# Sketched attention with a squared-ReLU feed-forward: four dummy matmuls ahead of the k features, w_o in rows of four, all casts of w_in on GpSimd

## The chip, the cores and the metric

The kernel runs on one core of a Trainium2 chip. The metric is device time in microseconds (us); of the kernel before there are three runs. A core has five engines that work side by side, each through its own queue in program order: TensorE (PE, with the weight loads shown as PEld), VectorE (DVE), ScalarE (ACT), GpSimd (POOL) and SyncE (SP, which here issues nearly all DMAs). They wait for each other by semaphores. SBUF is the core's working memory with 128 partitions, PSUM holds what PE writes.

## The reference

Attention with a degree-two sketch, then a feed-forward layer with a squared ReLU:

```python
# q, k, v: (4, 4, 1088, 32); S1, S2: (8, 32); w_in: (128, 2048); w_out: (2048, 128)
def phi(x):                       # 64 features of each row
    a = einsum('rd,bhsd->bhsr', S1, x)
    b = einsum('rd,bhsd->bhsr', S2, x)
    return einsum('bhsi,bhsj->bhsij', a, b).reshape(..., 64)
kv  = einsum('bhsf,bhsd->bhfd', phi(k), v)
z   = sum(phi(k), axis=2)
num = einsum('bhsf,bhfd->bhsd', phi(q), kv)
den = einsum('bhsf,bhf->bhs', phi(q), z)[..., None] + 1e-06
x   = (num / den).transpose(0, 2, 1, 3).reshape(4352, 128)
h   = maximum(x @ w_in, 0)
out = h * h @ w_out
```

The sum over the 2048 columns of h may be taken in any order, as long as column f of w_in meets row f of w_out.

## The kernel before

The feed-forward part is most of the work. The 4352 rows of x stand as columns of a tile xT (128 partitions are the model dimension). They are cut into ten chunks of 256 to 512 columns (FC). For each chunk and each of 16 blocks of 128 hidden features (d0 to d15) there is a first matmul pg (`ffn1`, L583: weights are a block of w_in, data are xT), a relu on ACT (L592, into gt), a square on ACT (L600) or DVE (L602, into g), and a second matmul that accumulates in PSUM (`ffn2`, L621, tile po; for the last chunk L616), whose weights are a block of w_o. Blocks are taken in units of one or more; the first chunk has the units u0 and u1 with one block each, then units of two blocks. po is transposed (L625) and stored by SP (L635).

The weights of both matmuls are loaded in four chunks of 512 columns: w_in arrives as float32 in w_in32 (`load_wi`, L204), and a cast (`cast_wi`, L665) writes it as the type that the matmul reads into w_in; w_o is loaded straight (`load_wo`, L209). Chunk c holds blocks 4c to 4c + 3. In w_o, block d of chunk c holds rows 128 (4c + d) to 128 (4c + d) + 127 of w_out, one row per partition, so each partition of a chunk's transfer takes four pieces of 128 floats (512 bytes). Casts 0, 1 and 3 stand ahead of the copies of the kv sums, cast 2 behind them; 0, 1 and 2 are on ACT, 3 is on POOL.

The attention part makes xT piece by piece. Batch 0 is written out by hand and comes first, in three pieces of q (256, 384 and 448 rows); the rest is placed by a planner (`_Order`) which fixes each engine's order when the kernel is built, from costs given for each step. The hand-written start goes like this:

- SP issues the loads of S1, S2, k, the first q, eight of v (L195), then w_in 0, w_o 0, the second q, and w_in and w_o 1 to 3 in turn, the third q, and batch 1's loads.
- PE does five dummy matmuls on constants (`keep_warm`, L672, W0 = 5), the sketch's selection (L683, tile sp), W1 = 2 more dummies, and then the k features kf (`a_kf`, L308), whose data come from DVE's transposes of k (L283). ACT copies half of each (L314), DVE multiplies them to kp (L324).
- PE makes the q features x (`q0`, L732) and sums kp and v into kvp (`a_kv0`, L384). DVE makes block-diagonal forms bd and zm from kvp (L764, L774), and PE the denominators den (L757, L787), and the numerators num (L787). From these DVE makes the first 256 columns of xT (L806 to L811).
- ACT copies kvp to kvt (L782), and a small product to sw (L798); PE replicates kvt (`a_rep`, L427), and ACT copies the result to kv (`a_rep_kv`, L433). After one more dummy (W3 = 1) PE starts on pg.

The second piece of q then goes through the planner's steps: qT (DVE, L289), qc (PE, L296), qt (DVE, L469), pd, dn and rc (DVE, L475, L485, L489), sixteen small copies rd (POOL, L497), shuffles qa and qb (DVE, L506), products qp (DVE, L521), nd (PE, L536), bc (DVE, L546) and xT (DVE, L553). Its 384 columns are the second chunk of the feed-forward part. kT (L277) and kc (L338) are the first steps of batch 1.

Of the kernel before, what the change touches and what calls it, by code (L numbers as in the profile page):

```python
# [14 lines left out]
def _ap(t: bass.AP, p0: int, np_: int, off: int, free):  # L15
    p = list(t.ap)[0]
    return bass.AP(
        t.tensor, t.offset + p0 * p[0] + off, [[p[0], np_]] + [list(d) for d in free]
    )
# [85 lines left out]
def kernel(  # L105
# [11 lines left out]
    nc = tc.nc  # L117
# [6 lines left out]
    NB = 16  # L124
    GT, G2, LA = 4, 6, 3.5
    LU = 4
    W0, W1, W3 = 5, 2, 1
    ND, QT, WI, KL, QL = 2, 3.0, (1.0, 1.9), (30.0, 12.0), 4.0


# [25 lines left out]
    def sb(name, cols, dt=F32, rows=128):  # L156
        return cpool.tile([rows, cols], dt, tag=name, name=name)
# [9 lines left out]
    w_in32, w_o, w_in = sb("w_in32", 2048), sb("w_o", 2048), sb("w_in", 2048, F32R)  # L167
# [39 lines left out]

    def load_wo(eng, c):
        eng.dma_start(  # L209
            _ap(w_o, 0, 128, 512 * c, [[128, 4], [1, 128]]),  # L210
            bass.AP(
                moe_w_out.tensor, moe_w_out.offset + c * 512 * 128,
                [[128, 128], [128 * 128, 4], [1, 128]],
            ),
        )

# [214 lines left out]
    def a_rep_kv(t_, col):  # L431
        kv = st[0, "kv"] = bpool.tile([128, 64 * H], F32, tag="kv", name="kv")
        nc.scalar.copy(  # L433
            _ap(kv, 0, 128, 0, [[32, 4], [128, 2], [1, 32]]),
            _ap(t_, 0, 128, col, [[512, 4], [64, 2], [1, 32]]),
        )
# [225 lines left out]
        store(1)  # L662

    def cast_wi(c):
        (nc.scalar.copy if c < 3 else nc.gpsimd.tensor_copy)(  # L665
            w_in[:, 512 * c : 512 * c + 512], w_in32[:, 512 * c : 512 * c + 512]
        )

    def keep_warm(n, cols=512):
# [16 lines left out]
    nc.scalar.copy(ss[:, :], sp[:, 0:80])  # L686
    load_wi(nc.sync, 0)
    load_wo(nc.sync, 0)
    load_q(nc.sync, 0, 256, 640)
    for c in range(1, 4):  # L690
        load_wi(nc.sync, c)
        load_wo(nc.sync, c)
# [75 lines left out]
            op=mult,  # L768
        )

    for c in (0, 1, 3):
        cast_wi(c)
    a_bd(1)
    nc.vector.tensor_tensor(  # L774
# [24 lines left out]
    nd0(num0, 0)  # L799
    a_rep(x0, 256)  # L800
    a_rep_kv(x0, 256)
    cast_wi(2)
    st["warm"] = psf.tile([128, 512], F32, tag="po", name="warm")
    keep_warm(W3)
    dT0 = wpool.tile([128, 256], F32, tag="dT0", bufs=1, name="dT0")
# [276 lines left out]
```

## Time and profile before

| what | value |
| --- | --- |
| median of 3 runs | 187.65 us (187.32 to 188.25) |
| the profiled execution, its own time | 188.6 us |
| its span | 186.8 us |
| DMA packets, bytes | 24673, 11.25 MB |
| of these under 512 B, under 2 KB | 18000, 23120 |
| cast of w_in, 128x512, on ACT | 0.62 us, three times |
| cast of w_in, 128x512, on POOL | 0.61 us, once |
| w_in transfers, issue to landing | 4.5 to 5.8 us, median 5.2 |
| w_o transfers, issue to landing | 4.7 to 6.2 us, median 5.3 |

A line of the timeline has its start and its length in us, the engine, the line of the kernel, the operation, the tile written and those read, the shape, and how many such operations are merged in it. What stands in brackets is the time for which the engine idled before, and what ended the wait. In the chain that ended last, each step is what released the next one. A record of PE's start-up shows two entries for each float32 matmul.

### The profile page before, as it was taken

To read this page: it belongs to the slowest core of one execution; us is meant where nothing else is said; L and a number is where in the kernel's file an instruction comes from. 1 tells how busy PE (TensorE), PEld (TensorE's weight loads), DVE (VectorE), ACT (ScalarE), POOL (GpSimd) and SP (SyncE) were. 2 spreads that over 40 slices of the span, in tenths; PEclk is the share of its full clock that TensorE was granted. 3 is DMA by queue.
4 is the path that set the end of the run, shared out by engine and by line. 5 is a ranking of instruction groups with operands and counts; after the bars stand their busy time and mean duration, and the time that the engine had idled before them with its cause. 6 is when DMAs were issued, how large, how long until landed. Compare 5 with 4: busy or idle time off the path is not lost.

```text
span 186.8 us, 3886 instructions
## 1 busy us (share of the span) xinstructions
PE 180.5 (97%) x1476; PEld 104.8 (56%) x1476; DVE 119.9 (64%) x254; ACT 136.5 (73%) x265; POOL 33.5 (18%) x154
## 2 busy tenths in 40 slices
PE   7987999999999999999999999999999999999992
PEld 1755866665656556554554555554555555555792
DVE  4856969996995679599626992999334235322420
ACT  3228977967986979499577875796778887877760
POOL 4401602608600000681000002830000000000000
PEclk9999999999999999999999999999999999999999
DMA  5879910110018810000492200002103000300111
GB/s 163 192 224 315 234 51 4 17 14 4 0 21 207 209 15 0 4 0 0 65 279 83 42 0 5 0 0 33 28 0 56 0 0 4 56 0 0 28 28 28
DMA packets 24673, 11.25 MB, mean 60 GB/s; under 512 B 18000, under 2 KB 23120, under 8 KB 24656
## 3 DMA queue, kind: packets, MB, share of 16 engines
q1 hardware_dynamic: 24448, 10.95, 25.0%
q8 instruction: 11, 0.18, 0.5%
q10 hardware_dynamic: 208, 0.07, 0.2%
q14 instruction: 6, 0.05, 0.1%
HBM read 8.78 MB, written 2.23 MB: 59 GB/s over the span
## 4 chain that ended last, share of the span: by engine, by line
PE 90%; SPq 3%; DMA 3%; ACT 1%; issue 1%; DVE 0%; ACTq 0%
PE po L621 60%; PE pg L583 18%; PE nd L536 3%; DMA w_in<-in_moe_w_in_dram 3%; PE kvp L402 2%; PE pol L616 2%; PE po L616 2%; SPq L195 2%; PE qc L296 1%; PE kc L338 1%; SPq L183 0%; SPq L177 0%; PE x L427 0%; ACT gt L592 0%; ACT w_in L665 0%
## 5 line engine op out<-in xcount | busy, mean ns | idle before, releaser
L621 PE MATMUL po<-g,w_o 128*128 128x512 f32 (+3 forms) x288 | 123.8, 548 | 0.0
L592 ACT ACTIVATE gt<-pg 128x512 f32<-128x512 f32 (+3 forms) x145 | 75.3, 569 | 33.1 <-PE pg L583 32.7
L621 PEld LDWEIGHTS po<-g,w_o 128*128 128x128 f32 x288 | 53.0, 189 | 32.4 <-issue 23.9
L583 PE MATMUL pg<-xT,w_in 128*128 128x512 f32 (+3 forms) x160 | 69.4, 517 | 0.5 <-ACT gt L592 0.5
L600 ACT ACTIVATE g<-gt 128x512 f32<-128x512 f32 (+2 forms) x105 | 60.0, 602 | 1.4
L602 DVE TENSOR_TENSOR g<-gt 128x512 f32<-128x512 f32 (+3 forms) x40 | 26.6, 667 | 41.9 <-ACT gt L592 41.3
L583 PEld LDWEIGHTS pg<-xT,w_in 128*128 128x128 f32 x160 | 29.0, 190 | 29.5 <-ACT gt L592 12.5
L443 POOL COPY kv<-kvt 32x64 f32<-32x64 f32 x48 | 12.1, 252 | 64.4 <-DVE kvt L420 62.3
L497 POOL COPY rd<-rc 32x9 f32<-32x9 f32 (+2 forms) x80 | 16.3, 203 | 12.5 <-DVE rc L489 9.1
L506 DVE STREAM_SHUFFLE qa<-qc 128x576 f32<-128x576 f32 (+2 forms) x20 | 11.6, 652 | 0.0
L521 DVE TENSOR_TENSOR qp<-qa,qb 128x576 f32<-128x576 f32 (+2 forms) x20 | 10.8, 605 | 0.0
L355 DVE TENSOR_TENSOR kp<-fs 128x576 f32<-128x576 f32 x12 | 8.4, 752 | 0.1
L469 DVE STREAM_TRANSPOSE qt<-qc 128x576 f32<-128x576 f32 (+2 forms) x10 | 5.8, 614 | 3.9 <-PE qc L296 3.9
L625 DVE STREAM_TRANSPOSE oT<-po 128x512 f32<-128x512 f32 (+3 forms) x9 | 5.9, 652 | 2.4 <-PE po L621 2.4
L536 PE MATMUL nd<-qp,kv 32*32 32x288 f32 (+2 forms) x320 | 6.8, 353 | 0.0
L553 DVE TENSOR_TENSOR xT<-nd,bc 128x576 fp32r<-128x576 f32 (+2 forms) x10 | 5.6, 601 | 1.0 <-PE nd L536 1.0
L546 DVE STREAM_TRANSPOSE bc<-rd 128x576 f32<-128x576 f32 (+2 forms) x10 | 5.8, 605 | 0.4 <-POOL rd L497 0.3
L506 DVE STREAM_SHUFFLE qb<-qc 128x576 f32<-128x576 f32 (+2 forms) x10 | 6.0, 650 | 0.0
L289 DVE STREAM_TRANSPOSE qT<-qn 128x192 f32<-128x192 f32 (+3 forms) x11 | 5.9, 563 | 0.0
L536 PEld LDWEIGHTS nd<-qp,kv 32*32 32x32 f32 x320 | 3.8, 103 | 3.7 <-issue 2.2
L616 PE MATMUL pol<-w_o,g 128*128 128x128 f32 x32 | 5.7, 275 | 0.0
L616 PE MATMUL po<-w_o,g 128*128 128x128 f32 x32 | 5.7, 275 | 0.0
(93 smaller groups left out, 90.7 us busy)
## 6 DMA issues: line engine op xcount, KB each, us to landing
kn<-in_k_dram SPq DMA_DIRECT2D x3, 544.0 KB, 5.5
qn<-in_q_dram SPq DMA_DIRECT2D x3, 544.0 KB, 7.9
vn<-in_v_dram SPq DMA_DIRECT2D x9, 144.0 KB, 4.8
w_in<-in_moe_w_in_dram SPq DMA_DIRECT2D x4, 256.0 KB, 5.2
w_o<-in_moe_w_out_dram SPq DMA_DIRECT2D x4, 256.0 KB, 5.3
out_dram<-oT SPq DMA_DIRECT2D x12, 64.0 KB, 2.0
out_dram<-oT SPq DMA_DIRECT2D x8, 56.0 KB, 2.8
out_dram<-oT SPq DMA_DIRECT2D x8, 48.0 KB, 1.8
```

The source lines that it names most:

```text
L355: nc.vector.tensor_tensor(out=_ap(st[b, "kp"], 0, 128, 64 * NT * h, [[64, NT], [8, 8], [1, 8]]), in0=_ap(fs, 0, 128, o, [[32, NT], [1, 8], ...
L443: nc.gpsimd.tensor_copy(_ap(st[b, "kv"], 32 * c, 32, 64 * h, [[32, E], [1, 32]]), _ap(st["kvt"], 32 * h, 32, 0, [[64, E], [1, 32]]),)
L497: nc.gpsimd.tensor_copy(st[b, "rd", i0][32 * h : 32 * h + 32, n * c : n * c + n], st["rc"][32 * c : 32 * c + 32, n * h : n * h + n],)
L506: nc.vector.stream_shuffle(in_=banks(st[b, "qc", i0], 2 * x, 0, m), out=_ap(st[b, which, i0], 0, 128, 2 * m * x, [[m, 2], [1, m]]), mask=m ...
L521: nc.vector.tensor_tensor(out=st[b, "qp", i0, e][:, r], in0=st[b, f"qa{e}", i0][:, r], in1=st[b, "qb", i0][:, r], op=mult,)
L536: nc.tensor.matmul(nd[32 * h : 32 * h + 32, 512 * c : 512 * c + m], kv[r, o : o + 32], qp[r, m * h : m * h + m], start=(e == 0), stop=(e = ...
L583: nc.tensor.matmul(st["pg", u][:, n * i : n * i + n], w_in[:, 128 * (d0 + i) : 128 * (d0 + i) + 128], xT[:, c0 : c0 + n],)
L592: nc.scalar.activation(gt[:, 0:w], st["pg", u][:, 0:w], Relu)
L600: nc.scalar.activation(g2[:, 0:w], gt[:, 0:w], Square)
L602: nc.vector.tensor_tensor(out=g2[:, 0:w], in0=gt[:, 0:w], in1=gt[:, 0:w], op=mult)
L616: nc.tensor.matmul(po[x // 128][:, 0:128], g[:, x : x + 128], w, start=(d == 0), stop=(d == NB - 1),)
L621: nc.tensor.matmul(po[0][:, 0:n], w, g, start=(d == 0), stop=(d == NB - 1))
```

## The change

Four dummy matmuls instead of two ahead of the k features. The load of w_o takes, in each chunk, four consecutive rows of w_out into each partition (2048 bytes in one piece), so that block j of chunk c holds the rows 512 c + 4 p + j on partition p. To match, the cast of w_in picks the columns 4 p + j of its chunk for block j: its source is read in steps of four floats, its target is written contiguously. All four casts are on GpSimd, in order, ahead of the copies of the kv sums. The order of the other instructions is the same on every engine.

```diff
-    W0, W1, W3 = 5, 2, 1
+    W0, W1, W3 = 5, 4, 1
...
     def load_wo(eng, c):
         eng.dma_start(
-            _ap(w_o, 0, 128, 512 * c, [[128, 4], [1, 128]]),
+            w_o[:, 512 * c : 512 * c + 512],
             bass.AP(
-                moe_w_out.tensor, moe_w_out.offset + c * 512 * 128,
-                [[128, 128], [128 * 128, 4], [1, 128]],
+                moe_w_out.tensor, moe_w_out.offset + c * 512 * 128, [[512, 128], [1, 512]]
             ),
         )
...
     def cast_wi(c):
-        (nc.scalar.copy if c < 3 else nc.gpsimd.tensor_copy)(
-            w_in[:, 512 * c : 512 * c + 512], w_in32[:, 512 * c : 512 * c + 512]
+        nc.gpsimd.tensor_copy(
+            _ap(w_in, 0, 128, 512 * c, [[128, 4], [1, 128]]),
+            _ap(w_in32, 0, 128, 512 * c, [[1, 4], [4, 128]]),
         )
...
-    for c in (0, 1, 3):
+    for c in range(4):
         cast_wi(c)
...
     a_rep(x0, 256)
     a_rep_kv(x0, 256)
-    cast_wi(2)
     st["warm"] = psf.tile([128, 512], F32, tag="po", name="warm")
```

## The prediction

> **What bounds the kernel now.** I read the page first (busy shares, then the chain that ended last), then that chain in order of time for the first 40 us, then the timeline of the first 24 us.
>
> ```profile
> span 186.8 us, 3886 instructions
> PE 180.5 (97%) x1476; PEld 104.8 (56%) x1476; DVE 119.9 (64%) x254; ACT 136.5 (73%) x265; POOL 33.5 (18%) x154
> PE 90%; SPq 3%; DMA 3%; ACT 1%; issue 1%; DVE 0%; ACTq 0%
> ```
>
> PE holds 90% of the chain; what isn't PE lies at the start. All three edits act before 20 us, so the question is how much earlier or later PE gets into its unbroken stream, and what in that stream could give it back. In the chain (start, length, what) the start looks like this:
>
> ```profile
> 7.83 5.74 DMA w_in<-in_moe_w_in_dram
> ...
> 13.59 0.02 ACT w_in L665
> ...
> 14.12 0.26 ACT kvt L782
> ...
> 15.14 0.38 ACT kv L433
> 15.52 0.52 ACT w_in L665
> 16.03 0.57 ACT gt L592 x2
> 16.60 0.04 issue
> 16.65 0.50 PE pg L583 x2
> ```
>
> The second w_in transfer lands at 13.57, ACT casts it (0.62 us), and only then copies kvt and kv, casts chunk 2 and does the first relu. The kv sums were ready for kvt at 11.4 (the end of the kvp matmuls, 8.85 + 2.54), so ACT stands 2.7 us late for a cast that isn't used before 16.65. That part of the chain goes. These are the lines of the timeline (start, duration, then what) for what is next:
>
> ```profile
> 3.42 1.03 PE L672 MATMUL warm<-const-bfloat16-1.0 128*128 128x512 bf16 x2
> 4.77 2.15 PE L308 MATMUL kf<-ss,kt 128*32 128x64 f32 x72 [0.31 <-DVE kt L283]
> 6.84 2.08 PE L732 MATMUL x<-qT,sq 64*128 64x256 f32 x8
> 11.32 0.65 PE L757 MATMUL den<-eps 1*64 1x256 f32 x4
> 17.68 0.61 POOL L665 CAST w_in<-w_in 128x512 fp32r<-128x512 f32 x1 [10.48 <-DMA w_in<-in_moe_w_in_dram]
> 17.70 0.70 DVE L475 TENSOR_TENSOR pd<-qt 128x96 f32<-128x96 f32 x1
> 18.81 0.23 DVE L489 RECIPROCAL rc<-dn 128x12 f32<-128x12 f32 x1
> 19.10 3.84 POOL L497 COPY rd<-rc 32x3 f32<-32x3 f32 x16 [0.81 <-DVE rc L489]
> 22.98 0.38 DVE L546 STREAM_TRANSPOSE bc<-rd 128x192 f32<-128x192 f32 x1 [0.33 <-POOL rd L497]
> 23.28 0.58 DVE L553 TENSOR_TENSOR xT<-nd,bc 128x192 fp32r<-128x192 f32 x2
> ```
>
> Two things are to be seen. First, a second chain runs beside PE: pd, dn, rc on DVE, sixteen rd copies on POOL, bc, xT. It ends at 23.86, and the first 384-column pg matmul, which needs that xT, starts at 24.04. So this chain has under 0.2 us of slack: whatever PE gains before, it keeps only as much as xT comes earlier. Second, pd took 0.70 us on 96 columns; later in the trace the same line takes 0.29 on 128. It began 0.02 us after the POOL cast and ended 0.11 after it: a DVE operation with two SBUF inputs waited for the POOL operation. A PSUM-reading one doesn't: six shuffles (L506) beside the rd copies follow each other every 0.28 us.
>
> **The change, part by part.** *Casts off ACT.* Three casts of 0.62 leave ACT. kvt can follow kvp at once (11.45), sw waits for the little x matmuls (end 12.73), the replicating matmuls L427 follow num (about 13.3 for 14.49), and the first relu no longer sits behind cast 2. For the first pg matmul xT (end 14.29) and cast 0 (start 11.50) are what is left: 14.35 for 14.97. The matmuls of u3, 16.65 before, would start behind qc (qT at 14.84, then 0.45): about 15.5. This is worth 1.1 us of PE by itself, if nothing takes it.
>
> *Casts on POOL.* POOL is idle from 7.2 to 17.68 and takes casts 0 to 2 in the landings' gaps, so their busy time costs nothing there; cast 3 was there already. Behind it in POOL's order stand only the sixteen rd copies. What changes is the cast's length C, since the source is now read with a step of 16 bytes. No row shows such a read. Below: the contiguous cast, 0.61. Above: the kv copies L443, 64 elements in 0.252, with nothing taken off for their fixed part 3.9 ns an element, 2.0 us. The nearest row is the memset of pd (L720), the only one stepped by the element (36 bytes): 36 elements in 0.16 against 0.10 for one element, 1.7 ns each, so C = 0.10 + 512 x 1.7 ns = 0.95. I take that.
>
> [...]
>
> *w_o in rows of 2 KB.* 512 packets of 512 B become 128 of 2 KB in each of four transfers. In the trace's packet records a 512 B packet takes 27 ns and a 2 KB one 84, so on each of 16 DMA engines 32 x 27 = 864 ns become 8 x 84 = 672: 0.19 us a transfer. The DMA share is about 1.0 from 13 to 18 us, so this counts there: two of these transfers are ahead of the last w_in chunk, which should land 0.38 earlier, at 17.3. SP issues the same number of transfers. The 2.49 us that it spends on the issue at 7.83 (0.43 to 0.50 elsewhere) is not explained by any row; bounds: it stays, or it goes and everything behind comes 2.0 earlier. I let it stay: the other three w_o transfers and what follows them are issued without such a stall.
>
> *Two more dummies.* Dummies follow each other every 0.43 us, so four end their issue at 3.42 + 1.71 = 5.13, and kf starts 0.36 late. Their gain can be the clock. Eight records of 256 columns take 2.08 us at 6.84 (0.26 each), four take 0.65 at 11.32 (0.16 with the tail): PE runs at about half speed early. The kvp records (L384; on average 282 ns from 8.9 to 9.5 us, 222 to 228 after) put the change near 9.4, 4.6 after PE's last idle gap, the 0.31 us at 4.77, which two more dummies close. Bounds: no change of that time, or unbroken work from 3.0, so full speed at 7.6. With the second, kf ends at 7.2, q0 at 8.45 instead of 8.85, kvp (72 records at 25 ns, the fast rate) at 10.3 instead of 11.39: xT 1.1 earlier, at 13.2. I take it as a little likelier than not.
>
> [...]
>
> *The sum.* With full speed at 7.6: xT 13.2, qc 14.3; cast 1 (13.4 to 14.35) holds the first two squares, which end at 15.1; qt to 15.75; cast 2 (15.1 to 16.05) holds pd to 16.3; rc 16.8. Cast 3 runs from 17.3 to 18.25, and rd starts at 18.3 instead of 19.10: the cover for rc's early end is cast 3 itself. xT comes 0.8 earlier, with part of the slack PE gets 0.85. After 24 us the stream is unbroken, so the span falls to 185.95; the profiled execution's own 188.6 lies 1.8 over its span, and I carry the same 0.85 to the median: 187.65 - 0.85 = **186.8**. With C = 0.61 it is 1.2 (186.45), with C = 2.0 cast 3 ends at 19.5 and, if pd slips in between two casts, it is -0.3 (187.95).
>
> **The rivals.** *The clock doesn't come earlier.* xT is then 0.25 late (14.55); cast 2 holds the squares until 16.1, qt ends at 17.5, and cast 3 (17.3 to 18.25) holds pd exactly as before: rc 19.0, rd 19.05. Gain 0.05 to 0.15: 187.5. For it: only one execution shows when the speed changed. Against: the idle gap is plainly there.
>
> *SP's long issue goes with the w_o packets.* The chunks land two us earlier, cast 3 is done by 17, rd follows rc at 16.9, and PE keeps 2.1: 185.5. For it: the stall comes right behind the first many-packet transfer. Against: the later ones, as above.
>
> *The strided cast is slow* (the slower side). The place is POOL before rd, the price C. With pd held by cast 3, rd starts at 17.3 + C + 0.81; it decides from C = 1.15 up. From 2.05 the casts (about 2.1 us between landings) stand in a row: c3 ends at 11.5 + 4C, at C = 2.0 rd starts at 20.3 and costs 1.05 (188.7), at C = 2.4 it ends at 21.1, rd 21.9, cost 2.65 (190.3). For it: nothing hides POOL there. Against: the memset row.
>
> **How the numbers follow.** Forecast 0.38, own range 186.3 to 187.4; clock no earlier 0.22; SP's stall gone 0.14; slow cast 0.26. What a measurement of this kernel can tell from no change is about 0.5%, 0.94 us. Faster by more: all of the stall case and some half of the forecast's, where C is small or the clock earlier still, 0.34. Slower by more: the slow cast, 0.25. The rest, 0.41, within. The range, 185.8 to 189.2, leaves out some 0.06 below and 0.13 above.
>
> **What would show it.** Right: L665 on POOL at 0.9 to 1.0 us, four times; kvt at 10.4 to 11.5; rd's copies starting at 18.2 to 18.5 right behind cast 3; the squares of u0 ending with a cast; some 1,536 fewer packets on q1; x<-qT,sq in about 1.3 us. Wrong: casts of 1.5 us or more, pd longer than 0.7, the long issue absent, kvp ending after 11.4, or idle time of PE appearing after 24 us, where I have none.

## The result, and the profile after

The changed kernel takes 187.55 us (median of 20 runs, 187.13 to 188.16), and the kernel before, measured beside it, 188.72 us (20 runs, 187.31 to 191.47): the ratio is 0.9938 with a 95% interval of 0.9912 to 0.9964. Measured again beside the experiments below it was 187.48 against 189.75, ratio 0.9919 (0.9882 to 0.9956). So it is faster, by 0.6 to 0.8%. The ratios leave out executions that took over 1.5% more than the fastest of their kernel (of before's 69 beside the experiments these are ten, all with a mean granted clock under 0.995), so they aren't the quotients of the medians. Two things stand out ahead of any trace: the changed kernel's median hardly moves between the two measurements while before's does by 1 us, and before's runs are spread over 4 us, the changed kernel's over 1.

The profiled execution is 1.3 us shorter than before's. From its page:

```profile
span 185.5 us, 3893 instructions
PE 179.4 (97%) x1478; PEld 103.6 (56%) x1478; DVE 120.7 (65%) x254; ACT 135.3 (73%) x262; POOL 37.3 (20%) x157
DMA packets 23138, 11.25 MB, mean 61 GB/s; under 512 B 18001, under 2 KB 21073, under 8 KB 23121
```

Some 1,535 packets are gone, as the longer rows of w_o make them. To the lines of before that the prediction shows, three are added here, two from its timeline and the last from its chain:

```profile
14.97 0.82 PE L583 MATMUL pg<-xT,w_in 128*128 128x256 f32 x4
16.35 0.76 DVE L602 TENSOR_TENSOR g<-gt 128x256 f32<-128x256 f32 x2 [1.51 <-ACT gt L592]
24.04 0.38 PE pg L583
```

These lines of the changed kernel's timeline (start, length, engine, line, what; most line numbers are lower by one) answer to them:

```profile
5.16 1.21 PE L307 MATMUL kf<-ss,kt 128*32 128x64 f32 x72
6.30 1.13 PE L732 MATMUL x<-qT,sq 64*128 64x256 f32 x8
10.41 0.27 ACT L782 COPY kvt<-kvp 128x128 f32<-128x128 f32 x1 [2.35 <-DVE bd L764]
10.91 1.11 POOL L664 CAST w_in<-w_in 128x512 fp32r<-128x512 f32 x1 [3.69 <-DMA w_in<-in_moe_w_in_dram]
12.74 0.71 PE L582 MATMUL pg<-xT,w_in 128*128 128x256 f32 x4 [0.38 <-DVE xT L810]
13.16 1.11 POOL L664 CAST w_in<-w_in 128x512 fp32r<-128x512 f32 x1 [1.14 <-DMA w_in<-in_moe_w_in_dram]
13.55 1.34 DVE L601 TENSOR_TENSOR g<-gt 128x256 f32<-128x256 f32 x2 [0.41 <-ACT gt L591]
15.20 1.11 POOL L664 CAST w_in<-w_in 128x512 fp32r<-128x512 f32 x1 [0.92 <-DMA w_in<-in_moe_w_in_dram]
15.48 0.95 DVE L474 TENSOR_TENSOR pd<-qt 128x96 f32<-128x96 f32 x1
16.77 1.13 POOL L664 CAST w_in<-w_in 128x512 fp32r<-128x512 f32 x1 [0.46 <-DMA w_in<-in_moe_w_in_dram]
16.83 0.23 DVE L488 RECIPROCAL rc<-dn 128x12 f32<-128x12 f32 x1
17.84 3.80 POOL L496 COPY rd<-rc 32x3 f32<-32x3 f32 x16
22.71 0.41 PE L582 MATMUL pg<-xT,w_in 128*128 128x384 f32 x1 [0.58 <-DVE xT L552]
```

Read from the top: kf and q0 run at full speed (kf in 1.21 us for 2.15, q0 in 1.13 for 2.08), kvt is copied at 10.41 instead of 14.12, and the first pg matmul starts 2.2 us earlier. Then the gain shrinks. The casts take 1.11 us each; the second holds the squares (1.34 us for two, 0.76 before), the third holds pd (0.95 us; it ends 0.12 after the cast), and the rd copies, whose rc was ready at 17.06, wait for the fourth until 17.84. That is 1.26 earlier than before, and the 384-column pg matmul follows 1.3 earlier, now waiting for xT. The span keeps just this 1.3.

### The profile page after: what moved, and what is told of

It is laid out like the page before. It is cut to its first block, busy times and chain, and to the rows that moved or that the text cites. A ratio compares the mean times of both kernels' runs of the same rounds, so it can differ in the third digit from the quotient of the medians.

```text
span 185.5 us, 3893 instructions
## 1 busy us (share of the span) xinstructions
PE 179.4 (97%) x1478; PEld 103.6 (56%) x1478; DVE 120.7 (65%) x254; ACT 135.3 (73%) x262; POOL 37.3 (20%) x157
## 4 chain that ended last, share of the span: by engine, by line
PE 86%; SPq 5%; DMA 3%; POOL 2%; issue 1%; DVE 0%
PE po L620 58%; PE pg L582 17%; PE nd L535 3%; DMA w_in<-in_moe_w_in_dram 3%; PE kvp L401 2%; PE pol L615 2%; PE po L615 2%; SPq L195 2%; POOL rd L496 2%; SPq L204 2%; PE qc L295 1%; PE kc L337 1%; SPq L209 1%; POOL w_in L664 1%; SPq L183 0%
## 5 line engine op out<-in xcount | busy, mean ns | idle before, releaser
L601 DVE TENSOR_TENSOR g<-gt 128x512 f32<-128x512 f32 (+3 forms) x40 | 27.2, 681 | 40.8 <-ACT gt L591 40.2
L664 POOL CAST w_in<-w_in 128x512 fp32r<-128x512 f32 x4 | 4.5, 1116 | 6.2 <-DMA w_in<-in_moe_w_in_dram 6.2
```

Source lines behind the costliest of these rows:

```text
L601: nc.vector.tensor_tensor(out=g2[:, 0:w], in0=gt[:, 0:w], in1=gt[:, 0:w], op=mult)
```

## The experiments

All are timed beside the kernel before, in three series with executions of before in each; before's medians are 189.79 (series of e1, e2, e3, e5), 189.75 (a_again, e8, e9, e7) and 188.72 (e4 and the three repeats). Shown with each is its difference from before or from the changed kernel.

**e1: the dummies alone.**

```diff
-    W0, W1, W3 = 5, 2, 1
+    W0, W1, W3 = 5, 4, 1
```

> The kernel before with four dummies instead of two, nothing else. If full speed comes earlier because PE no longer pauses ahead of kf: x<-qT,sq lasts about 1.1 us instead of 2.08 and kvp ends near 9.7 instead of 11.4 in the profile. Theory (the dummies pay only together with the casts off ACT): kvt still stands behind cast 1 on ACT, which waits for a landing near 13.6, so the first pg matmul stays near 14.9 and the span near 186.7; what may go is the long executions, those above 189. Rival (the dummies alone bring it): kvt at 10.4, first pg near 13, span near 185.5.

188.99 us (12 runs), ratio 0.9973 (0.9937 to 1.0009): no difference that can be told. q0 took 1.13 us, so full speed came early, but the span of the profiled execution was 187.0: that brought nothing. The long executions didn't go. The profile shows why. PE's timeline behind the pause (what stands in brackets is the idle time before and its end):

```profile
14.04 0.50 PE L427 MATMUL x<-kvt,irep 32*128 32x128 f32 x8 [2.24 <-ACT sw L798]
14.52 0.82 PE L583 MATMUL pg<-xT,w_in 128*128 128x256 f32 x4
```

And the stretches of one us behind it (busy share and count of PE, PEld, DVE, ACT, POOL, then granted clock, DMA share, GB/s):

```profile
14.00:15.00 1.00, 0.96 (x11) 0.81 (x13) 0.00 (x0) 0.31 (x2) 0.00 (x0) 1.00 1.00 307
15.00:16.00 1.00, 0.89 (x35) 0.41 (x34) 0.10 (x1) 1.00 (x4) 0.04 (x1) 0.65 1.03 345
16.00:17.00 1.00, 0.81 (x3) 0.81 (x4) 1.00 (x3) 0.97 (x3) 0.79 (x1) 0.50 0.96 391
17.00:18.00 1.00, 1.00 (x4) 0.82 (x4) 0.89 (x4) 0.77 (x2) 0.00 (x0) 0.50 1.09 284
18.00:19.00 1.00, 1.00 (x6) 0.88 (x5) 0.94 (x6) 0.69 (x2) 0.34 (x2) 0.65 1.05 192
```

PE gets to the replication of kvt earlier, but kvt still stands behind ACT's second cast, so PE idles for 2.24 us. Soon after, its granted clock falls to half from about 15.3 to 18.7, just when the feed-forward part begins. Eleven of e1's twelve executions have a mean granted clock under 0.995. (Before's profile gives the granted clock as 1.00 from the start, although its q0 takes 2.08 us, where the changed kernel's takes 1.13; so the mean clock shows such falls, not the slow start.) The kernel before has a clock under 0.995 in most of its executions too, though not in the profiled one. Of the 59 that the ratios use:

| mean granted clock | executions of before | median us | range |
| --- | --- | --- | --- |
| 0.995 and more | 19 | 188.13 | 187.11 to 189.11 |
| 0.985 to 0.995 | 20 | 188.82 | 187.98 to 189.65 |
| under 0.985 | 20 | 189.90 | 189.34 to 190.28 |

By an estimate from this profile, 3.4 us at half clock (15.3 to 18.7) take 0.01 off a mean over some 187 us (its own is 0.988), so these should be executions with no such fall, one, and two. The nine of e1 with one fall have a median of 188.93, where before's have 188.82: at the same clock, too, the dummies alone bring nothing. Of 32 executions of the changed kernel the lowest mean clock is 0.996.

**e3 and e3_again: all casts on POOL, contiguous, nothing else.**

```diff
-        (nc.scalar.copy if c < 3 else nc.gpsimd.tensor_copy)(
+        nc.gpsimd.tensor_copy(
...
-    for c in (0, 1, 3):
+    for c in range(4):
         cast_wi(c)
...
-    cast_wi(2)
```

> The kernel before with all four casts on POOL in order, contiguous, nothing else (two dummies, w_o in pieces of 512 B). Theory: casts of 0.61 us; kvt directly behind kvp; cast 3 still starts when its chunk lands near 17.7 and holds pd to 18.3, so rd starts near 19.05 and the span is within 0.2 of before's 186.8. Rival (ACT's cast is what bound the kernel): first pg 0.5 to 1 us earlier and the span 0.6 to 1.0 shorter.

> All casts on POOL, contiguous, two dummies, w_o in pieces of 512 B, a second time: 187.0 to 187.6, spread over 2 us, none with a mean clock under 0.995; this is the part of the change that does most, 2 us or more under before's median here.

187.18 us (6 runs), ratio 0.9875 (0.9837 to 0.9913), and 187.30 (12 runs), ratio 0.9936 (0.9903 to 0.9969). No execution is under 0.995 in clock. The first expectation, nearly no gain, is wrong, and its rival, a span 0.6 to 1.0 shorter, held. The profiled span, 186.2 for an expected 186.6 to 187.0, shows little of it, since this was the longest of the six executions; the median span is 185.3 and 185.2, and that of before's executions which keep their clock 186.3. In time that is 0.8 to 1.0 under their 188.13; the rest of the difference is the executions of before whose clock falls. The second expectation holds for the median, not for the 2 us under before's, which were 1.4.

**e2 and e2_again: the changed kernel with two dummies.**

```diff
-    W0, W1, W3 = 5, 4, 1
+    W0, W1, W3 = 5, 2, 1
```

> The changed kernel with two dummies instead of four. Theory: full speed comes later again (x<-qT,sq about 2 us in most executions), pd is held by cast 3 (16.8 to 17.9), rd starts near 18.7 instead of 17.84, so the span is 0.8 to 0.9 over the changed kernel's, near 186.3, and the spread of the runs is as wide as before's. Rival (casts off ACT bring it alone): span 185.5, rd at 17.9, runs as close together as the changed kernel's.

> The changed kernel with two dummies, a second time. Theory (what brings the median down is the casts off ACT, the dummies add some tenths by making full speed come early in every execution): 187.3 to 188.2, with executions up to 188.7 that the changed kernel with four lacks, none with a mean clock under 0.995. Rival (the dummies bring it): 188.5 or more.

187.32 us (6 runs), ratio 0.9892 (0.9854 to 0.9930), and 187.49 (12 runs), ratio 0.9946 (0.9919 to 0.9973). That is the changed kernel's 187.55 and 187.48: there the two dummies bring nothing that can be measured, so the first expectation's theory (0.8 to 0.9 longer) missed and its rival held; the second came out. In e2's profile full speed came early without them (q0 in 1.13 us), in e2_again's late (1.79).

**e5 and e5_again: e3 with four dummies,** so the changed kernel without the rows of w_o and without the stepped read.

> Casts on POOL, contiguous, and four dummies; w_o in pieces of 512 B as before. Theory: casts of 0.61 us and full speed early; chunk 3 lands near 17.3 to 17.7 and is cast by 18.2, rd right behind it near 18.2, so the span is 0.8 to 0.9 below before's: near 186.0. That would leave 0.4 us to the rows of w_o, by the earlier landing less the longer cast. Rival (the rows of w_o bring nothing, their cast costs 0.5): span 185.3 or less, rd at 17.5 or earlier.

> The same with four dummies, a second time: 186.3 to 186.6 and within 1 us of each other, so 0.6 to 1.0 under e3_again and about 1.0 under the 187.5 that the changed kernel took in both of its measurements. Rival (the first time was luck of where full speed came): 186.9 or more.

186.42 us (6 runs), ratio 0.9829 (0.9801 to 0.9857), and 186.89 (12 runs), ratio 0.9906 (0.9874 to 0.9939). Both medians are under those of both kernels (against the changed kernel by 0.6 to 1.1, from different series). The first expectation's theory, a span near 186.0, missed, and its rival, 185.3 or less with rd at 17.5 or earlier, held. Against e3 in the same series e5 is 0.76 and 0.41 lower, but the intervals overlap, and the second expectation (186.3 to 186.6) was missed by 0.3: that the dummies help here is likely, not settled. POOL's timeline in e5:

```profile
16.15 0.61 POOL L665 CAST w_in<-w_in 128x512 fp32r<-128x512 f32 x1 [0.77 <-DMA w_in<-in_moe_w_in_dram]
16.71 3.75 POOL L497 COPY rd<-rc 32x3 f32<-32x3 f32 x16
```

The rd copies start 1.13 us earlier than in the changed kernel, and the span is 1.2 shorter, 184.3.

**e9: the changed kernel with contiguous casts.** The rows of w_o stay in fours. The kernel leaves out the matching order of w_in, so rows of w_out meet the wrong columns, and only its time is of use.

```diff
-            _ap(w_in, 0, 128, 512 * c, [[128, 4], [1, 128]]),
-            _ap(w_in32, 0, 128, 512 * c, [[1, 4], [4, 128]]),
+            w_in[:, 512 * c : 512 * c + 512], w_in32[:, 512 * c : 512 * c + 512]
```

> The changed kernel with contiguous casts: the rows of w_o stay in fours, the columns of w_in are not permuted to match, so the sums over the hidden features pair the wrong rows and columns. Theory: casts 0.61 us for 1.11; cast 3 ends half a us earlier and rd follows at the earlier of that and rc, median 0.4 to 0.9 below the changed kernel's (near 186.7 to 187.0). Rival (the length of the cast is hidden by the landings): median within 0.2 of the changed kernel's.

186.41 us (6 runs), ratio 0.9859 (0.9804 to 0.9915): 1.07 under the changed kernel in the same series, more than the 0.4 to 0.9 expected. The two intervals against before overlap, but five of its six runs lie below the lowest of the changed kernel's twelve. The stepped read costs about this; without it, the longer rows of w_o leave the time where e5 has it (186.42 and 186.89, from other series), so these bring no gain that can be told. In its profile rd waits for rc, not for a cast:

```profile
16.44 3.83 POOL L496 COPY rd<-rc 32x3 f32<-32x3 f32 x16 [0.22 <-DVE rc L488]
```

**a_again: the changed kernel beside e9, e8 and e7.**

> The changed kernel again, beside the three that follow. Theory: PE's pause in the middle of the start is gone, so no execution has a mean granted clock under 0.995, and the median is near 187.5, whatever before does on this chip; the executions of before with a clock near 0.98 are 1.5 to 2 us longer than those at 1.0. Rival (the clock of before is chance, and as likely here): some executions of this kernel at 0.98 too.

187.48 us (12 runs, 186.78 to 188.20), lowest mean clock 0.996, while 11 of the 17 executions of before that this series adds to the table are under 0.995. Its profiled execution, at 188.20 the longest of the twelve, shows another way in which the stepped cast costs time:

```profile
13.08 3.62 POOL L664 CAST w_in<-w_in 128x512 fp32r<-128x512 f32 x3 [2.14 <-DMA w_in<-in_moe_w_in_dram]
14.54 2.44 DVE L601 TENSOR_TENSOR g<-gt 128x256 f32<-128x256 f32 x2 [0.41 <-ACT gt L591]
18.54 3.83 POOL L496 COPY rd<-rc 32x3 f32<-32x3 f32 x16 [1.83 <-DVE rc L488]
```

Three casts stand in a row, the first two squares last 2.44 us instead of before's 0.76, and rd waits for DVE's chain: it starts at 18.54, 0.7 later than in the other profile of this kernel.

**e8: before, with PE's pause filled.**

```diff
     nd0(num0, 0)
+    st["warm"] = psf.tile([128, 512], F32, tag="po", name="warm")
+    keep_warm(5)
     a_rep(x0, 256)
     a_rep_kv(x0, 256)
     cast_wi(2)
-    st["warm"] = psf.tile([128, 512], F32, tag="po", name="warm")
     keep_warm(W3)
```

> The kernel before with five more dummies on PE between num and the replication of kvt, which PE reaches at 13.3 and starts at 14.5; all casts where they were, two dummies ahead of kf, w_o in pieces of 512 B. Theory (the long executions of before come from PE's pause behind ACT's casts, which lets its clock fall): no or few executions under 0.99, median near the short executions of before, 187.7 to 188.3, 1.5 us under before's median. Rival (the time lost is the late kvt itself): median as before's or longer, by up to 0.5 us.

188.68 us (12 runs), ratio 0.9972 (0.9934 to 1.0010). Ten of twelve executions keep their clock, where before's do in 6 of 17, so PE's idle time here has a part in the fall. The profiled execution is one of the other two. There the dummies leave a pause of 1.42 us:

```profile
14.68 0.50 PE L427 MATMUL x<-kvt,irep 32*128 32x128 f32 x8 [1.42 <-ACT sw L798]
```

Its clock is at half from about 16.8 (0.89 in the stretch 16 to 17, 0.50 in the next two); if this fall is as long as e1's, an estimate, it ends at 20.2. Over the same 3.4 us ahead of the fall PE was busy for 1.68 us (13.36 to 16.78); ahead of e1's it was 1.25 (11.88 to 15.29). Around its pause of 1.19 us, before's profile has 2.20 (12.78 to 16.19), and there the clock doesn't fall.

The time is a miss: the median is 1.07 under before's, not 1.5, the interval includes no change, and what keeps its clock still takes 188.6, about 0.5 over the executions of before that do (188.13). Where that goes is open: in the profile the dummies end before the pause, so they don't hold the replication up.

**e4: the rows of w_o and the stepped read, casts on before's engines.**

```diff
... (load_wo as in the change)
         (nc.scalar.copy if c < 3 else nc.gpsimd.tensor_copy)(
-            w_in[:, 512 * c : 512 * c + 512], w_in32[:, 512 * c : 512 * c + 512]
+            _ap(w_in, 0, 128, 512 * c, [[128, 4], [1, 128]]),
+            _ap(w_in32, 0, 128, 512 * c, [[1, 4], [4, 128]]),
         )
```

> The kernel before with the rows of w_o in fours and the casts' source stepped to match; casts on the engines and at the places of before, two dummies. Theory: the casts on ACT stay near 0.62 us or get longer, kvt stays behind cast 1, and most executions keep the fall of the clock (mean granted clock 0.98 to 0.99): median within 0.6 of before's, 189.2 to 190.4. Rival (the shorter packets of w_o were what held the start): median 1 us or more under before's.

190.37 us (6 runs), ratio 1.0113 (1.0054 to 1.0173): slower, and by more than the 0.6 expected against the 188.72 of this series. Five of six executions are under 0.995. The operations on w_in in its profile (shortest, median and longest in ns, first and last start):

```profile
L664 ACT CAST w_in<-w_in x3: 1105/1107/1126, 11.1 to 15.2; 128x512 fp32r<-128x512 f32 x3
L664 POOL CAST w_in<-w_in x1: 1356/1356/1356, 16.6 to 16.6; 128x512 fp32r<-128x512 f32 x1
```

The step costs ACT as much as POOL, 0.49 us a cast, and on ACT the first two stand ahead of kvt.

**e7: e5 with the w_in transfers moved ahead.**

```diff
-    for c in range(1, 4):
-        load_wi(nc.sync, c)
-        load_wo(nc.sync, c)
+    load_wi(nc.sync, 1)
+    load_wi(nc.sync, 2)
+    load_wo(nc.sync, 1)
+    load_wi(nc.sync, 3)
+    load_wo(nc.sync, 2)
+    load_wo(nc.sync, 3)
```

> Contiguous casts on POOL, four dummies, w_o in pieces of 512 B, and the order of the transfers changed to w_in 1, w_in 2, w_o 1, w_in 3, w_o 2, w_o 3. Theory (the landing of chunk 3 with its cast and the sixteen rd copies sets when PE's unbroken stream begins): chunk 3 lands 0.5 to 0.8 earlier, rd begins at 16.0 right behind rc, median 185.9 to 186.2, against 186.42 measured for the same kernel with the transfers in turn. Rival (something else sets it, such as qT or a w_o chunk that now comes late): 186.4 or more.

186.58 us (6 runs), ratio 0.9873 (0.9817 to 0.9928): no better than e5, so the theory missed and the rival held. Cast 3 started at 15.62, but rc was only ready at 16.97, so in this execution DVE's chain set the start of rd. One of the six has a mean clock of 0.989 (188.05 us), the only one under 0.995 among 98 executions with all casts on POOL: casts off ACT make the fall rare, not impossible.

## Why the prediction came out as it did

The time on record, 186.8, is 0.75 under the 187.55 measured, within the range; the gain, 0.85, was 1.17. The way there was right in the profile and incomplete for the median.

That the two gains lie this close is partly luck. Among executions that keep their clock the median span fell from 186.3 (before's 19) to 185.5, close to the 0.85 foreseen. Some 0.2 of it doesn't reach the time: outside the span before takes 1.8 us and the changed kernel 2.0. Every kernel here with all casts on POOL takes 1.9 to 2.1 there (medians), those with casts on ACT 1.8 to 1.9; no trace shows why. That leaves 0.6 (188.13 to 187.55). The other 0.6 of the 1.17 is the executions of before whose clock falls.

- **Casts off ACT.** Right as a step: kvt stands directly behind the kv sums, and the first pg matmul starts at 12.74, where e1, with the same early clock and the casts on ACT, has it at 14.52. It was priced at what the profiled execution showed, a PE that waits. That the clock can fall behind such a wait isn't in that profile, whose clock stays at 1.00, and the prediction had no term for it. This is the step that failed, "I carry the same 0.85 to the median: 187.65 - 0.85": one execution without a fall of the clock, and the median of three runs, stood for a kernel whose median is 188.7 to 189.8 over 17 to 29 runs. In the profiles of e1 and e8 the clock fell to half behind pauses of 2.24 and 1.42 us; behind before's 1.19 us it stayed at 1.00.
- **The stepped cast.** The place was right in the profiled execution (POOL before rd, cast 3 as the cover) and the size too small: 1.11 us where 0.95 was taken. What it costs was mis-sized more: 0.35 between C = 0.61 and 0.95 in the sum, 1.07 between e9 and the changed kernel. A longer cast also holds the squares (1.34 us for 0.76) and pd (0.95 for 0.70), and in a_again's profile three casts stand in a row at 1.21 each already, not only from the 2.05 foreseen.
- **pd behind a cast.** Right, and seen twice more: pd took 0.95 beside cast 2, the squares 1.34.
- **Longer rows of w_o.** Cast 3 started 0.91 earlier; 0.57 of it is SP's issue, which came 0.57 earlier (11.30 for 11.87), the rest is close to the 0.38 foreseen. But e9 against e5 shows no time won.
- **Two more dummies.** Foreseen for 7.6 us, full speed was there by kf in the profiled execution, at 5.2 to 6.4 (that the clock might come "earlier still" had a part in the chances, but no run had shown it); in a_again's kf still took 2.13, and only q0, from 7.29, was fast. In the seven profiles with four dummies q0 took 1.13 to 1.14; in the seven with two it took 1.13 to 2.08, four of them under 1.2. So the dummies seem to do what was said, which fourteen profiles can't settle. kvp took 2.32 us at full speed (32 ns a record) where the sum had 1.85 (at 25). What fell is the dummies' worth: the sum let nearly all of the gain hang on it, with 0.05 to 0.15 without it, and e2 without them takes no longer than the changed kernel. In e2_again's profile cast 3 ends at 18.6 and rd follows at once, so there cast 3 covers the difference as the sum had it; in e2's it doesn't.
- **The rivals.** Slow cast: in the changed kernel 1.11 is below its point of 1.15, but put on ACT (e4) the same step makes the kernel slower. SP's long issue didn't go in the changed kernel (2.09 us at 7.73; in a_again's profile 1.46 us at 9.17). The clock not coming earlier was priced at 187.5, and e2 and e2_again take 187.3 and 187.5, but that is a gain over before's real median, not the 0.05 to 0.15 foreseen, and in e2's profile the clock came early all the same.
- **After 24 us** PE's stream kept what it had gained, as assumed.

## What to carry to other kernels

Look at the spread of the runs and the mean clock of each before costing anything: a profile of a good execution hides what the others lose. A copy that waits for a transfer doesn't belong ahead of one that PE needs in the same engine's order: in e1 it left PE a pause of 2.24 us, the first pg matmul started at 14.52 for the changed kernel's 12.74, and the clock fell to half behind it. Where a layout shortens a transfer's list of packets, cost the operation that undoes it too; here that was 0.5 us a cast, and the shorter list brought nothing that could be told.

## What was not expected

A cast that reads every fourth float takes 1.11 us for 0.61 to 0.62, on ACT and POOL alike. POOL can be held up beside DVE as DVE beside POOL: e4's cast on POOL took 1.36 us and the first two squares beside it 1.69, where the changed kernel's profile has 1.11 and 1.34 and before's squares, with no cast beside them, took 0.76. SP's one long issue, 1.1 to 2.6 us, moved among the q, w_in and w_o transfers from profile to profile (at 7.26 in e3, 7.73 in the changed kernel, 9.33 in e5), and with it chunk 3's landing. Its cause stays open.
